# FAVOR attention and a bilinear FFN on one core: weights fetched by another queue, the second addend of a weight product added by VectorE, and a re-ordered lead-in

## The chip, the cores and the metric

The kernel runs on one core of one Trainium2 chip. The metric is the device time of one launch in microseconds (us). The engines are TensorE (PE; its weight loads are shown apart as PEld), VectorE (DVE), ScalarE (ACT), GpSimd (POOL) and SyncE (SP). SP does no arithmetic here: it only issues DMAs. ACT does arithmetic and issues some DMAs too. A queue issues its DMAs in the order of the program, and one that has to wait holds up those behind it.

## The reference

The reference is attention with random features, followed by a feed-forward product with a bilinear gate. There are 8 batches of 8 heads, 576 tokens, 64 numbers per head and 128 features.

```python
def phi(x):                                   # x = q or k, scaled by 1/64**0.25
    proj = np.einsum('bhsd,md->bhsm', x, omega)
    h = proj - np.sum(x * x, axis=-1, keepdims=True) / 2.0
    return np.exp(h - np.max(h, axis=-1, keepdims=True)) / np.sqrt(m)
kv = np.einsum('bhsm,bhsd->bhmd', phi(k_s), v)
z = np.sum(phi(k_s), axis=2)
num = np.einsum('bhsm,bhmd->bhsd', phi(q_s), kv)
den = np.einsum('bhsm,bhm->bhs', phi(q_s), z)[..., None] + 1e-06
x = (num / den).transpose(0, 2, 1, 3).reshape(4608, 512)
out = (((x @ w1) * (x @ w2)) @ w3) @ w_out    # w1, w2: 512x1024; w3: 1024x1024; w_out: 1024x512
```

The four weight matrices arrive as 64-bit floats, q, k, v and omega as 32-bit floats.

## The kernel before, in words

**Tiling.** The 4608 tokens are 36 chunks of 128. For a chunk, `k_chunk` makes the features of k and `kv_batch` sums them with v once all chunks of a batch are there (tile `kvp`). `q_chunk` makes the features of q (projection `qpj`, exponential `qe`, fp16 pair `eq`) and has them transposed by DMA (`eqT`). `q_attend` multiplies them by `kv` (tile `nu`) and divides; `x_turn` makes a pair of fp16 numbers of the row and has it transposed by DMA (`xT`). `gate` computes `x@w1` and `x@w2` (tile `ab`) and their product, and `project_out` multiplies by W (tile `o`) and stores. W = w3·w_out is computed once on the chip, in fp32 (`W_block`, tile `wp`): 1024 rows in eight blocks, and since w_out arrives in two parts of 512 rows, W's first halves of the sums are kept in `Wb` and the second halves are added later. That addition is a matmul of the kept block by a unit matrix, `ident`, into the same sum (L616); ACT then copies the sum back (L630).

**Precision.** An fp32 matmul shows as two records in the profile. Elsewhere numbers go as pairs of fp16 (a high and a low part) in three passes (`PASSES`). The first five chunks of q and the first ten of k (`QF`, `KF`) are projected in fp32 whole, L287; later ones are first split into pairs.

**The weights' lead-in.** The 20 units of weights (the letters of `ORDER`: o is w_out, W is w3, 1 and 2 are w1 and w2; a, b and S are the splits that follow) hold 1 MB each. A unit takes these steps: the fetch, a DMA of ACT's queue (L526); the magnitude, an Abs on ACT (L534); the bits, four operations on DVE that put a 32-bit float together from the two words (L540, L542, L543, L545); and then the product on PE with its copy (`W`), or the sums of magnitudes (`1`, `2`). There are three buffers for raw words, so the fetch of a unit waits until the bits of the unit three earlier are done, and two buffers for magnitudes.

**What sets the order.** A plan of slots. Each chunk begins three slots after the one before (`PACE`), each piece is put into a slot with a rank (`put`), `PER` says how many steps of the weights go into a slot, `LAGS`, `KVD`, `KOFF`, `VB`, `NOFF` and `QOFF` shift single pieces, and `RESERVE` is the number of units of gates that are held back as filling. The framework then orders the instructions of each engine by the order in which they were written and by when it thinks their inputs are there. `EH`, `EL`, `QH`, `QL` and `DQ` pick engines for the high and low parts and the form of the exponential (for one form, '1', eight small operations with the maximum as bias on ACT; for '0', one addition on DVE and one exponential). At its start the program loads omega (L205, L206, into the first block of `Wb`), two chunks of k and, soon, two of q, all by SP's queue (L228). The rows of v come by SP's queue as well (L351), and so do the transposes (L427, L481).

## The time and the profile before

| | |
|---|---|
| three runs | 848.72, 844.92 and 849.43 us; median 848.72 us |
| the profiled execution | 844.82 us, of which the span is 843.0 us |
| mean granted clock of TensorE | 0.977 |
| PE busy | 786.0 us, 93% of the span |
| DVE busy | 577.0 us, 68% |
| ACT busy | 437.6 us, 52% |
| POOL busy | 228.5 us, 27% |
| the first output projection begins | 187.65 us |

The rows of the profile are read thus. A group has its line, engine, operation and tiles, the number of instructions, then their busy time in us and the mean of one in ns, and behind the next bar the idle time of the engine just before them, with what ended it. A row of the timeline has the start and the length in us, then engine, line, operation, tiles and the number of instructions run together, and in brackets the idle time before. A row of the windows has the two ends and the length of the stretch, then for PE, PEld, DVE, ACT and POOL the busy us with the instructions in parentheses, then TensorE's granted clock, the busy share of the DMA engines and the GB/s that they moved.

### The profile page before, as it was taken

The numbers are of one execution on the slowest core, as the hardware profiler recorded it, in microseconds if no ns is written. First come the engines' busy times: TensorE is split into PE (matmuls) and PEld (weight loads), VectorE is DVE, ScalarE is ACT, GpSimd is POOL, SyncE is SP. The second block draws the span as 40 slices with busy tenths as digits, with TensorE's granted clock in tenths as the row PEclk, the third lists the DMA queues.
The fourth block names the chain that finished last, engine by engine and source line by source line (L and its number), as shares of the span: only waits on it lengthen the run. The fifth ranks groups of instructions, "written<-read, shape, count | busy, mean of one in ns | idle before, by whom it ended". The sixth has DMA issues, their size and how long they took to land.

```text
span 843.0 us, 19911 instructions
## 1 busy us (share of the span) xinstructions
PE 786.0 (93%) x8353; PEld 580.1 (69%) x8353; DVE 577.0 (68%) x1049; ACT 437.6 (52%) x793; POOL 228.5 (27%) x210
## 2 busy tenths in 40 slices
PE   1968799799979999999999999999999999999998
PEld 1436455696858777777777777777777777777773
DVE  5695967886888788768777877787778765452000
ACT  2674746884655557656555565466545433232221
POOL 0000001221435324533333334333433332221110
PEclk8889699999989999999999999999999999999999
DMA  8584659334435454535343634354333342321000
GB/s 302 187 267 145 200 151 213 89 64 72 114 93 115 73 153 89 101 76 126 91 87 81 137 85 87 79 126 101 78 84 67 65 85 66 76 51 38 26 14 37
DMA packets 142521, 88.38 MB, mean 105 GB/s; under 512 B 116704, under 2 KB 116832, under 8 KB 142432
## 3 DMA queue, kind: packets, MB, share of 16 engines
q1 hardware_dynamic: 134944, 66.15, 35.8%
q10 hardware_dynamic: 7488, 20.97, 7.6%
q8 instruction: 65, 1.06, 0.5%
q14 instruction: 24, 0.20, 0.1%
HBM read 49.35 MB, written 9.44 MB: 70 GB/s over the span
## 4 chain that ended last, share of the span: by engine, by line
PE 46%; DVE 16%; ACT 9%; issue 7%; DMA 1%; POOL 1%; SPq 0%; DVEq 0%; ACTq 0%; POOLq 0%
PE ab L678 24%; PE o L707 15%; DVE nm L306 3%; PE kvp L411 3%; DVE khl L155 2%; DVE ke L320 2%; PE nu L440 2%; DVE qe L320 2%; ACT ek L143 2%; ACT qe L321 1%; PE qpj L294 1%; DVE xs L455 1%; DMA kraw<-kT 1%; DVE asb L688 1%; ACT xhl L476 1%
## 5 line engine op out<-in xcount | busy, mean ns | idle before, releaser
L678 PE MATMUL ab<-xT,w12b 128*128 128x256 f16 (+1 forms) x3840 | 390.7, 262 | 5.7 <-DMA xT<-xhl 4.7
L678 PEld LDWEIGHTS <-w12b 128*128 128x128 f16 x3840 | 340.1, 98 | 43.5 <-issue 4.9
L707 PE MATMUL o<-Wb,arena 128*128 128x512 f16 x864 | 195.7, 383 | 1.0 <-DVE p2p L195 1.0
L693 POOL TENSOR_TENSOR arena<-asb,arena 128x512 f16<-128x512 f32 x72 | 92.8, 1288 | 316.0 <-ACT arena L692 316.0
L707 PEld LDWEIGHTS <-arena 128*128 128x128 f16 x864 | 82.3, 98 | 98.1 <-issue 4.2
L688 DVE TENSOR_TENSOR asb<-ab,asb 128x512 f32<-128x512 f32 x72 | 49.5, 687 | 115.9 <-PE ab L678 91.8
L330 POOL TENSOR_TENSOR eq<-qe,eq 128x1024 f16<-128x1024 f32 x34 | 74.5, 2192 | 135.0 <-DVE eq L141 80.6
L618 PE MATMUL wp<-w12b 128*128 128x512 f32 x128 | 64.6, 656 | 12.5 <-DVE w12b L545 12.4
L330 POOL TENSOR_TENSOR ek<-ke,ek 128x1024 f16<-128x1024 f32 x26 | 56.6, 2179 | 70.9 <-ACT ek L143 62.5
L692 ACT CAST arena<-asb 128x512 f16<-128x512 f32 x72 | 44.1, 612 | 58.0 <-DVE asb L688 57.9
L155 DVE SCALAR_TENSOR_TENSOR qhl<-qraw,s,qhl 128x512 f16<-128x512 f32 x31 | 51.4, 1657 | 18.1 <-ACT qhl L152 18.1
L687 ACT ACTIVATE asb<-ab 128x512 f32<-128x512 f32 x72 | 42.3, 587 | 34.7 <-PE ab L678 30.9
L321 ACT ACTIVATE qe<-qe,ln_e,es 128x1024 f32<-128x1024 f32 x31 | 38.4, 1238 | 41.2 <-DVE qe L320 41.1
L321 ACT ACTIVATE ke<-ke,ln_e,es 128x1024 f32<-128x1024 f32 x26 | 32.2, 1238 | 51.1 <-DVE ke L320 51.1
L476 ACT ACTIVATE xhl<-xs,p2r 128x512 f16<-128x512 f32 x36 | 26.0, 721 | 62.1 <-DVE p2r L198 60.3
L618 PEld LDWEIGHTS wp<-w12b 128*128 128x128 f32 x128 | 26.2, 210 | 45.7 <-issue 30.7
L306 DVE TENSOR_REDUCE nm<-kpj 128x8 f32<-128x1024 f32 x36 | 43.8, 1217 | 9.8 <-PE kpj L287 5.1
L711 ACT ACTIVATE o<-o,oscs 128x512 f32<-128x512 f32 x36 | 24.3, 675 | 40.8 <-PE o L707 33.6
L411 PE MATMUL kvp<-vhl,ek 128*128 128x65 f16 (+1 forms) x880 | 41.8, 208 | 3.4 <-DVE xs L455 3.4
L306 DVE TENSOR_REDUCE nm<-qpj 128x8 f32<-128x1024 f32 x36 | 43.7, 1215 | 0.2
L440 PE MATMUL nu<-kv,eqT 128*128 128x65 f16 (+1 forms) x960 | 34.1, 195 | 8.4 <-DMA eqT<-eq 7.6
L141 DVE CAST eq<-qe 128x1024 f16<-128x1024 f32 x31 | 21.5, 692 | 29.0 <-ACT qe L321 29.0
(121 smaller groups left out, 929.2 us busy)
## 6 DMA issues: line engine op xcount, KB each, us to landing
kraw<-kT SPq DMA_DIRECT2D x36, 256.0 KB, 2.8
qraw<-qT SPq DMA_DIRECT2D x36, 256.0 KB, 2.7
vraw<-v SPq DMA_DIRECT2D x36, 256.0 KB, 4.3
out<-o SPq DMA_DIRECT2D x36, 256.0 KB, 2.3
arena<-w3T ACTq DMA_DIRECT2D x8, 1024.0 KB, 6.5
arena<-w ACTq DMA_DIRECT2D x8, 1024.0 KB, 6.2
arena<-wo ACTq DMA_DIRECT2D x4, 1024.0 KB, 5.1
eqT<-eq SPq DMA_TRANSPOSE x72, 3.1
```

The lines of the kernel that those rows point to most:

```text
L155: nc.vector.scalar_tensor_tensor(lo, src, s, hi, ALU.mult, ALU.subtract)
L306: nc.vector.tensor_reduce(nm, pj, AX.X, ALU.max, negate=True)
L321: nc.scalar.activation(e, e, AF.Exp, scale=es, bias=ln_e)
L330: (nc.vector if lo == "d" else nc.gpsimd).tensor_tensor(t[:, 1], e, t[:, 0], ALU.subtract)
L411: nc.tensor.matmul(ps[:, h // 4, h % 4], x, y, start=n == 0, stop=n == len(mm) - 1)
L440: nc.tensor.matmul(nu[r0:r1, h // 4, h % 4], t[:, x, place(h), r0:r1], kvs[b][:, y, h], start=n == 0, stop=n == 2,)
L618: nc.tensor.matmul(ps, w[:, j, k * P : (k + 1) * P], guest[:, j], start=j == j0, stop=j == HALF - 1,)
L678: nc.tensor.matmul(ps[:, k], w12[m][i][cc][:, a, r * P : (r + 1) * P], x[:, b, cc, off : off + T], start=j == 0, stop=j == len(mm) - 1,)
L688: nc.vector.tensor_tensor(asb, ab[1], asb, ALU.mult)
L692: nc.scalar.copy(h[:, 0], asb)
L693: nc.gpsimd.tensor_tensor(h[:, 1], asb, h[:, 0], ALU.subtract)
L707: nc.tensor.matmul(ps, hs[c, f][0][:, a], W[f][:, b], start=i == 0, stop=i == len(mm) - 1)
```

## The change

1. **Fetches.** The 20 fetches of weights are issued by SP's queue (`FQ = 's'`). The first unit, of w_out, is fetched in two DMAs, and its Abs and its bits are done in halves (`cuts`). The loads of k's chunks 0 and 1 are issued by ACT's queue instead.
2. **Early Abs.** An Abs of one column is the first arithmetic of ACT (`T0`).
3. **Omega** has a tile of its own, and its split is put into slot 0 instead of slot 4 (`OM_AT`).
4. **W's second addend** is added by DVE, straight from the sum to `Wb` (`WADD`): the eight matmuls by `ident` and eight of the sixteen copies on ACT go.
5. **v's scaling** (ten operations) goes from DVE to ACT (`V_ACT`).
6. **Whole projections**: q's chunk 5 and k's chunk 10 are projected in fp32 as well (`QF`, `KF`).
7. **Order**: q's first two loads wait for the second unit's bits (`QD`); priorities for pieces (`PR`); and new tables `PER`, `PACE`, `LAGS`, `KVD`, `KOFF`, `VB`, `NOFF`, `QOFF` and `RESERVE`, with the tables that pick engines. `MS`, `KFIRST` and `OM1` stand at values that change nothing.

```diff
-EH = 'aaaaaadadadada'
-EL = 'ddddddpdpdppppp'
-QH = 'aaaaad'
-QL = 'ddp'
-DQ = '111110000000'
-QF = 5
-KF = 10
-V_ACT = 0
+EH = 'aaaaaddadaaadaaaaaaaaaa'
+EL = 'ddppddpdpddpppppppppppppppp'
+QH = 'aaaaaaddd'
+QL = 'ddpdppppppppppp'
+DQ = '101110010000000000000000000'
+QF = 6
+KF = 11
+V_ACT = 1
+PR = {'vscale': 100, 'norm': 400, 'split': 100, 'bits': -100, 'x': 50}
+START = 1
+WADD = 1
+FQ = 's'
+T0 = 1
+CH = 1
+QD = 1
...
-PER = [3, 1, 0, 1, 0, 1, 1, 0, 1, 0, 1, 1, 0, 1, 1, 0, 0, 1, 1, 1, 1, 1, 1, 1, 1, 1, 1, 1, 1, 1, 1, 1, 1]
-PACE = {13: 2}
+PER = [3, 1, 0, 1, 0, 1, 1, 0, 1, 0, 1, 1, 0, 1, 1, 0, 0, 1, 1, 1, 1, 1, 1, 1, 0, 3, 0, 1, 1, 1, 1, 1, 2]
+PACE = {13: 3, 11: 3}
...
-RESERVE = 3
+RESERVE = 2
...
-OM_AT = 4
+OM_AT = 0
...
-    om_raw = Wb[:, 0, 0:M]
-    nc.sync.dma_start(om_raw[0:D], omT)
-    nc.sync.dma_start(om_raw[D:P], omT)
+    om_raw = const.tile([P, M], F32, name="om_raw")
+    if OM1 == 0:
+        nc.sync.dma_start(om_raw[0:D], omT)
+        nc.sync.dma_start(om_raw[D:P], omT)
...
+    if T0:
+        nc.scalar.activation(om_sq, ln_e, AF.Abs)
...
-    def load(src, c, name):
+    def load(src, c, name, queue=nc.sync):
...
-        nc.sync.dma_start(t, src[c])
+        dma = queue.dma_start(t, src[c])
...
+        if name == "q" and c < 2 and QD >= 0:
+            tc.add_manual_dep(
+                dma.ins,
+                converted[QD].name,
...
-            nc.scalar.dma_start(raw.rearrange("p (j i) -> p j i", j=src.shape[1]), src)
-            st["raw"] = raw.rearrange("p (i t) -> p i t", t=2)
+            raw = raw.rearrange("p (j i) -> p j i", j=src.shape[1])
+            step = src.shape[1] // cuts
+            for k in range(0, src.shape[1], step):
+                {'a': nc.scalar, 's': nc.sync, 'p': nc.gpsimd}[pick(FQ, nfetch[0])].dma_start(raw[:, k : k + step], src[:, k : k + step])
...
-            nc.scalar.activation(st["g"], st["raw"][:, :, 1].bitcast(F32), AF.Abs)
+            for a in pieces:
+                nc.scalar.activation(st["g"][:, a], st["raw"][:, a, 1].bitcast(F32), AF.Abs)
...
-        return from_float64(lambda: dst, src, f"wo_{j}")
+        return from_float64(lambda: dst, src, f"wo_{j}", cuts=1 if n or not START else 2)
...
-                if j0:
+                if j0 and not WADD:
                     nc.tensor.matmul(ps, ident, Wb[:, i + k + 1], start=True, stop=False)
...
-                nc.scalar.copy(Wi, ps)
+                if j0 and WADD:
+                    nc.vector.tensor_tensor(Wi, ps, Wi, ALU.add)
+                else:
+                    nc.scalar.copy(Wi, ps)
...
-    for u in units[:RAW64_BUFS]:
+    for n, u in enumerate(units[:RAW64_BUFS]):
         u[0]()
         u[0] = None
+        if START and n < 2:
+            load(kT, n, "k", nc.scalar)
...
-    for c in range(2):
+    for c in range(0 if START else KFIRST, 0 if START else 2):
         load(kT, c, "k")
```

Three places show how the tables and queues move instructions. The first is SP's queue from the start of the program (`kraw`, `qraw` and `vraw` are the loads of a chunk of k, q and v; `arena` holds the raw weights). Before:

```order
L205 DMA Wb<-omT 64x128
L206 DMA Wb<-omT 64x128
L228 DMA kraw_104<-kT 128x512
L228 DMA kraw_106<-kT 128x512
L228 DMA qraw_338<-qT 128x512
L228 DMA qraw_359<-qT 128x512
L228 DMA kraw_163<-kT 128x512
L228 DMA kraw_210<-kT 128x512
L351 DMA vraw_176<-v 128x512
```

and now:

```order
L226 DMA om_raw<-omT 64x128
L227 DMA om_raw<-omT 64x128
L568 DMA arena<-wo 128x1024 x2
L568 DMA arena<-wo 128x2x1024
L568 DMA arena<-w3T 128x4x512
L568 DMA arena<-w 128x2x1024
L257 DMA kraw_155<-kT 128x512
L568 DMA arena<-w3T 128x4x512
L387 DMA vraw_184<-v 128x512
```

Here the weights have moved into the same line as k, q and v: the fetch of the fourth unit (w) stands ahead of the third load of k, and that load ahead of the fifth unit.

The second place is DVE in the middle of the lead-in: `kpj` is the projection of a chunk of k, `vhl` the scaled v, L155 (L175 now) the low half of a split of w1, `ws` its scale. The first row before is the last step of the seventh unit, and what follows lies ahead of the eighth:

```order
L545 SCALAR_TENSOR_TENSOR w12b<-arena 128x1024
L306 TENSOR_REDUCE nm<-kpj_316 128x8
L388 TENSOR_SCALAR vhl_1_340<-vraw_178,s_3_283 128x8x64
L316 TENSOR_SCALAR nm<-nm 128x8
L388 TENSOR_SCALAR vhl_2_361<-vraw_180,s_3_283 128x8x64
L388 TENSOR_SCALAR vhl_3_374<-vraw_182,s_3_283 128x8x64
L155 SCALAR_TENSOR_TENSOR w12b<-w12b,ws 128x512
L306 TENSOR_REDUCE nm<-kpj_378 128x8
L388 TENSOR_SCALAR vhl_4_400<-vraw_184,s_3_283 64x8x64
```

Now (the two L592 are the last steps of the eighth and of the ninth unit):

```order
L342 TENSOR_REDUCE nm<-kpj_321 128x8
L215 TENSOR_SCALAR p2p_4_300<-l1m 128x1
L592 SCALAR_TENSOR_TENSOR w12b<-arena 128x1024
L218 RECIPROCAL p2r_4_302<-p2p_4_300 128x1
L352 TENSOR_SCALAR nm<-nm 128x8
L584 TENSOR_SCALAR arena<-arena 128x1024
L638 TENSOR_SCALAR ws<-p2r_4_302 128x1
L586 TENSOR_SCALAR arena<-arena 128x1024
L589 SCALAR_TENSOR_TENSOR arena<-arena 128x1024
L175 SCALAR_TENSOR_TENSOR w12b<-w12b,ws 128x512
L592 SCALAR_TENSOR_TENSOR w12b<-arena 128x1024
```

The scalings of v are gone from between the units, and three of the four low halves of the split and one of the two reductions of `kpj` have moved behind the ninth unit; before, all four halves and both reductions stood ahead of the eighth unit's last step.

The third place is PE ahead of the first gate (`wp` is a block of W, `qpj` and `kpj` the projections of a chunk of q and of k, `ab` the gate). Before:

```order
L618 MATMUL wp_0_675<-w12b 128x512 x2
L287 MATMUL kpj_651<-Wb,kraw_387 128x128 x8
L618 MATMUL wp_0_675<-w12b 128x512 x2
L618 MATMUL wp_1_681<-w12b 128x512 x4
L287 MATMUL qpj_816<-Wb,qraw_488 128x128
L678 LDWEIGHTS w12b
L678 MATMUL ab_0_0_693<-xT_619,w12b 128x128
```

and now:

```order
L670 MATMUL wp_0_664<-w12b 128x512
L670 MATMUL wp_1_669<-w12b 128x512 x4
L323 MATMUL qpj_813<-om_raw,qraw_496 128x128 x8
L323 MATMUL kpj_853<-om_raw,kraw_526 128x128 x8
L670 MATMUL wp_0_694<-w12b 128x512 x4
L670 MATMUL wp_1_699<-w12b 128x512 x4
L733 LDWEIGHTS w12b
L733 MATMUL ab_0_0_710<-xT_690,w12b 128x128
```

Two projections and a second pair of W's blocks now stand between the first pair and the gate; before, that pair came behind the gate.

More of the change, by code (lines that the diff above doesn't have):

```diff
@@ L1 @@
 import math
-from contextlib import ExitStack
+from contextlib import ExitStack, nullcontext
 import concourse.bass as bass
@@ L114, in tile_favor_attention_then_bilinear_ffn, with ahead, early, go @@
     TOK = GROUP * P
+    def ahead(kind):
+        return tc.high_priority(offset=PR[kind]) if PR.get(kind) else nullcontext()
+    def early(kind, fn):
+        def go(*args):
+            with ahead(kind):
+                return fn(*args)
+        return go
     const = ctx.enter_context(tc.tile_pool(name="const", bufs=1))
@@ L339, in k_chunk @@
             ek[c] = e
-        if c == 0:
+        if c == 0 and K_BEHIND >= 0:
             with tc.issue_after(converted[K_BEHIND]):
@@ L533, in magnitude, with words @@
             st["dst"] = new()
-            nc.scalar.activation(st["g"], st["raw"][:, :, 1].bitcast(F32), AF.Abs)
-        def bits():
-            g = st["g"]
-            top, low = st["raw"][:, :, 1], st["raw"][:, :, 0]
-            nc.vector.tensor_scalar(g, g, F64_TOP, F64_LEAST, ALU.min, ALU.max)
-            g = g.bitcast(U32)
-            nc.vector.tensor_scalar(g, g, 3, 0x3FFFFFFF, ALU.logical_shift_left, ALU.bitwise_and)
-            nc.vector.scalar_tensor_tensor(g, top, 0xC0000000, g, ALU.bitwise_and, ALU.bitwise_or)
-            converted.append(
-                nc.vector.scalar_tensor_tensor(
-                    st["dst"].bitcast(U32), low, 29, g, ALU.logical_shift_right, ALU.bitwise_or
-                ).ins
-            )
+            for a in pieces:
+                nc.scalar.activation(st["g"][:, a], st["raw"][:, a, 1].bitcast(F32), AF.Abs)
+        def words():
+            for a in pieces:
+                g, dst = st["g"][:, a], st["dst"][:, a].bitcast(U32)
+                top, low = st["raw"][:, a, 1], st["raw"][:, a, 0]
+                nc.vector.tensor_scalar(g, g, F64_TOP, F64_LEAST, ALU.min, ALU.max)
+                g = g.bitcast(U32)
+                nc.vector.tensor_scalar(
+                    g, g, 3, 0x3FFFFFFF, ALU.logical_shift_left, ALU.bitwise_and
+                )
+                nc.vector.scalar_tensor_tensor(
+                    g, top, 0xC0000000, g, ALU.bitwise_and, ALU.bitwise_or
+                )
+                last = nc.vector.scalar_tensor_tensor(
+                    dst, low, 29, g, ALU.logical_shift_right, ALU.bitwise_or
+                )
+            return last
+        def bits():
+            with tc.issue_after(converted[-1]) if 0 < len(converted) < CH else nullcontext():
+                last = words()
+            converted.append(last.ins)
             raw_at.append(st["at"])
             mag_at.append(st["mag"])
-        return [fetch, magnitude, bits]
+        return [fetch, early("mag", magnitude), early("bits", bits)]
     l1s = {}
@@ L621, in product @@
                         guest[:, j],
-                        start=j == j0,
+                        start=j == (0 if WADD else j0),
                         stop=j == HALF - 1,
@@ L636, in W_block @@
             product,
-            keep,
+            early("keep", keep),
         ]
@@ L723, in v_batch @@
         cs = chunks_of(b)
-        v_work.extend((b, lambda n=n: v_norm(b, n)) for n in range(len(cs)))
-        v_work.append((b, lambda: v_scale(b)))
-        v_work.extend((b, lambda n=n: v_split(b, n)) for n in range(len(cs)))
+        v_work.extend((b, early("vnorm", lambda n=n: v_norm(b, n))) for n in range(len(cs)))
+        v_work.append((b, early("vscale", lambda: v_scale(b))))
+        v_work.extend((b, early("vsplit", lambda n=n: v_split(b, n))) for n in range(len(cs)))
     def v_unit():
@@ L761, in tile_favor_attention_then_bilinear_ffn @@
         units.append([None] * 3 + st + [None] if len(st) == 1 else st + [None] * (5 - len(st)))
-    for u in units[:RAW64_BUFS]:
+    for c in range(KFIRST):
+        load(kT, c, "k")
+    for n, u in enumerate(units[:RAW64_BUFS]):
         u[0]()
         u[0] = None
+        if START and n < 2:
+            load(kT, n, "k", nc.scalar)
     behind = sorted(range(5), key=lambda k: -SKEW[k])
@@ L791, in ready @@
     def ready(c):
-        x_turn(c)
+        early("x", x_turn)(c)
         for c0, m in groups:
@@ L797, in ready @@
                     need = [(n, u // m) for n in range(2)]
-                    units.append((need, lambda c0=c0, m=m, u=u: gate(c0, m, u)))
+                    units.append((need, early("gate", lambda c0=c0, m=m, u=u: gate(c0, m, u))))
                 for k, f in enumerate(behind_by):
                     units.insert(2 + 3 * k, f)
-                behind_by[:] = [(["k"], lambda c=c: project_out(c)) for c in range(c0, c0 + m)]
+                behind_by[:] = [
+                    (["k"], early("out", lambda c=c: project_out(c))) for c in range(c0, c0 + m)
+                ]
                 queue.extend(units)
```

54 lines of the change are left out of this document (35 added, 19 removed).

## The prediction, as put on record

> **What bounds the kernel now.** I read the windows first, cut where the work changes: the start, the weights up to the first kv sum, the stretch to the first gate, from there to the first output projection, and the rest. Columns: the ends and length of the stretch, busy us of PE, PEld, DVE, ACT and POOL, TensorE's granted clock, DMA share, GB/s.
>
> ```profile
> 0.00:21.50 21.50, 3.51 (x33) 3.33 (x33) 12.45 (x27) 5.03 (x6) 1.43 (x12) 0.87 0.89 303
> 21.50:77.00 55.50, 47.52 (x198) 26.49 (x199) 40.39 (x62) 34.93 (x78) 0.52 (x1) 0.90 0.58 196
> 77.00:106.50 29.50, 19.89 (x115) 11.28 (x115) 26.51 (x43) 19.34 (x49) 0.47 (x5) 0.77 0.68 208
> 106.50:187.60 81.10, 75.17 (x798) 56.47 (x797) 60.40 (x126) 57.23 (x129) 12.47 (x15) 1.00 0.58 130
> 187.60:300.00 112.40, 105.10 (x1374) 80.37 (x1375) 91.00 (x169) 64.95 (x108) 40.15 (x34) 0.97 0.46 98
> 300.00:760.00 460.00, 455.53 (x5263) 347.40 (x5262) 336.66 (x607) 240.32 (x398) 163.06 (x134) 1.00 0.42 89
> ```
>
> From 300 us on PE is busy for 455.5 of 460 us: what is won earlier is kept there, and nothing more can be won. Up to 187.6 us PE is idle for 41.5 us: 18.0 in the start, 8.0, 9.6 and 5.9 in the next three. Both orders have issued the same work of PE by the first output projection, but for eight matmuls; so the sum is made at that one milestone, 187.65 us. The timeline gives the marks on the way and the groups of the first 188 us the durations.
>
> ```profile
> 8.86 0.69 DVE L540 TENSOR_SCALAR arena<-arena 128x1024 f32<-128x1024 f32 x1 [7.78 <-ACT arena L534]
> 21.54 9.42 PE L618 MATMUL wp<-w12b 128*128 128x512 f32 x16 [8.36 <-DVE w12b L545]
> 40.14 1.60 PE L287 MATMUL kpj<-Wb,kraw 64*128 64x128 f32 x22
> 62.16 7.13 PE L618 MATMUL wp<-w12b 128*128 128x512 f32 x16 [2.17 <-DVE w12b L545]
> 69.13 8.15 PE L411 MATMUL kvp<-vhl,ek 128*128 128x65 f32 x72
> 88.41 0.29 PE L440 MATMUL nu<-kv,eqT 128*128 128x65 f16 x2 [6.63 <-DMA eqT<-eq]
> 106.56 5.52 PE L678 MATMUL ab<-xT,w12b 128*128 128x128 f16 x96 [2.34 <-DMA xT<-xhl]
> 187.65 1.25 PE L707 MATMUL o<-Wb,arena 128*128 128x512 f16 x5
> ```
>
> Until 62 us PE waits for the last step of the bits on DVE, L545: the first block of W at 21.54, the fourth (ninth unit) at 62.16. After that it waits for transposes: 6.63 us for `eqT`, 2.34 us for `xT`.
>
> ```profile
> L618 PE MATMUL wp<-w12b 128*128 128x512 f32 x128 | 64.6, 656 | 12.5 <-DVE w12b L545 12.4
> L616 PE MATMUL wp<-Wb,ident 128*128 128x512 f32 x16 | 8.4, 616 | 0.0
> L540 DVE TENSOR_SCALAR arena<-arena 128x1024 f32<-128x1024 f32 x20 | 14.4, 719 | 17.8 <-ACT arena L534 17.8
> L542 DVE TENSOR_SCALAR arena<-arena 128x1024 uint32<-128x1024 uint32 x20 | 13.8, 690 | 0.4
> L543 DVE SCALAR_TENSOR_TENSOR arena<-arena 128x1024 uint32<-128x1024 uint32 x20 | 24.4, 1220 | 0.4
> L545 DVE SCALAR_TENSOR_TENSOR w12b<-arena 128x1024 uint32<-128x1024 uint32 x20 | 24.3, 1220 | 6.2 <-PE wp L618 5.9
> L306 DVE TENSOR_REDUCE nm<-kpj 128x8 f32<-128x1024 f32 x10 | 12.2, 1217 | 5.1 <-PE kpj L287 5.1
> L155 DVE SCALAR_TENSOR_TENSOR w12b<-w12b,ws 128x512 f16<-128x512 f32 x16 | 12.1, 757 | 2.5 <-ACT w12b L152 2.5
> L388 DVE TENSOR_SCALAR vhl<-vraw,s 128x512 f32<-128x512 f32 (+1 forms) x10 | 4.4, 478 | 0.1
> L581 DVE TENSOR_REDUCE l1m<-l 128x1 f32<-128x512 f32 x4 | 2.7, 684 | 0.0
> L316 DVE TENSOR_SCALAR nm<-nm 128x8 f32<-128x8 f32 x14 | 2.3, 164 | 0.0
> ```
>
> One unit's bits take 0.719 + 0.690 + 1.220 + 1.220 = 3.85 us of DVE.
>
> **The lead-in's order: −5 us.** Before, DVE does this from 8.86 us to the end of the ninth unit, 62.1 us: nine units 34.6, five reductions of `kpj` 6.1, one `l1m` 0.7, four low halves of a split 3.0, five scalings of v 2.4, and some 20 small operations like L316, 0.15 us each, 3.0: 49.8 of 53.3 us, so 3.5 us of waits. Now the scalings are ACT's, three of the halves and one reduction stand behind the ninth unit: 34.6 + 4.9 + 0.7 + 0.8 + 3.0 = 44.0 us. With the same start and the same waits the ninth unit ends at 8.9 + 44.0 + 3.5 = 56.4 us. Behind it on PE stand its product, 7.1 us, and 80 records of the kv sum; before, 72 took 8.15 us, so 80 take 9.1: it ends at 72.6 us instead of 77.3, 4.7 us sooner. PE sets a second bound. Its first block of W now comes behind a third projection of k, and by the order of DVE after three units, two reductions and three steps of the fourth: 8.9 + 11.5 + 2.4 + 2.6 = 25.4 us instead of 21.5. From there it has the 47.5 us of the second window less the projection done ahead (1.60 us for 22 records, so 1.2 for 16), 46.3: 71.7 us. Both bounds lie close; I take −5. If DVE's waits vanish PE binds, −5.6; if 5 us of waits are added, 0.
>
> **The start: 0.** The early Abs and the half-sized first unit would bring DVE's start of 8.86 us forward.
>
> ```profile
> 6.41 1.28 ACT L534 ACT_TABLE_LOAD   x1 [6.41 <-DMA arena<-wo]
> 7.71 1.12 ACT L534 ACTIVATE arena<-arena 128x1024 f32<-128x1024 f32 x1
> 10.54 0.29 ACT L169 ACTIVATE junk_om<-Wb 128x128 bf16<-128x128 f32 x1
> ```
>
> The table's load is 1.28 us, half an Abs 0.56: −1.8 us. Omega's split now stands ahead of the bits and costs about that much again: a Square of 0.29 us on ACT, a small matmul, and on DVE five operations, four of them small like L316. I keep 8.9 us, with −1.8 and +1 as bounds.
>
> **W's second addend: −6.9 us.** Sixteen records of L616 go. Warm, their weight loads follow each other by 0.43 us:
>
> ```profile
> 126.07 0.19 PEld L616 LDWEIGHTS wp<-Wb,ident 128*128 128x128 f32 x1 [0.24 <-issue]
> 126.50 0.19 PEld L616 LDWEIGHTS wp<-Wb,ident 128*128 128x128 f32 x1 [0.24 <-issue]
> L688 DVE TENSOR_TENSOR asb<-ab,asb 128x512 f32<-128x512 f32 x5 | 3.4, 687 | 5.1 <-PE ab L678 5.1
> ```
>
> 16 × 0.43 = 6.9 us, on an engine that is 93% busy in the fourth window, where 12 of the 16 stand; the busy time of the group, 8.4 us, is the upper bound. In their place come eight additions of the kind of L688, 8 × 0.69 = 5.5 us, while the scalings of v take 4.4 us off DVE: 1.1 us more in all. The cover is DVE's idle time, 110.6 − 86.9 = 23.7 us in the third and fourth windows. A block's banks come free after DVE's addition instead of ACT's copy; what stands ahead of that addition is at most a unit's remaining steps, and if half of the eight wait for one of 1.2 us with nothing beside them, the saving is 4.
>
> **From the kv sum to the first output projection: −3 us.** PE's idle time there is 15.5 us. Ahead of the first `nu` (6.63 us of waiting) stands one more projection of q, 1.2 us. Between the first pair of blocks and the gate now stand two projections and eight products more, so the 2.34 us for `xT` are filled. −3.5, and 0.5 back because the first gate's fillers are then missing further on. Bounds: −5 (half of what is left), and +4 if a transpose is late by one unit's bits, since SP's queue now holds weights.
>
> **After it: 0.** One more chunk of q and one of k are projected in fp32: 16 records, 1.2 us, where 24 of fp16 stood, 1.5 us by the 20 below; I count nothing for it. One wait of 3.7 us stands there, and the new tables may remove or repeat it: with the smaller waits beside it −5 to +6.
>
> ```profile
> 243.32 0.28 PE L294 MATMUL qpj<-om,qhl 64*128 64x128 f16 x4 [3.67 <-ACT qhl L152]
> 245.77 1.25 PE L294 MATMUL kpj<-om,khl 64*128 64x128 f16 x20 [0.68 <-DVE mx L468]
> ```
>
> **The fetches: 0 by themselves**, since DVE, not the landing, ends PE's waits up to 62 us. What they cost ACT:
>
> ```profile
> L526 ACTq DMA_DIRECT2D arena<-w3T x8: 374/374/418, 6.0 to 101.0; - x8
> 14.25 3.07 SPq L351 DMA_DIRECT2D vraw<-v  x5
> 14.32 0.39 ACTq L526 DMA_DIRECT2D arena<-w  x1
> 23.03 1.12 ACT L534 ACTIVATE arena<-arena 128x1024 f32<-128x1024 f32 x1 [7.60 <-DMA arena<-w]
> ```
>
> 0.37 us an issue, 7.5 us for all twenty, on an engine busy for 116.5 of the first 187.6 us. The fourth unit, issued at 14.32 together with five loads of v, is there at 23.0. The Trainium skill (DMA: Bandwidth & Descriptors, Issuing engines are not separate DMA queues) says that DMAs started by different engines run on the same 16 DMA engines, and that another issuer saves only the issuing. The DMA share of 0.89 in the first window agrees; by that rule edit 1 is worth 0 on the path, as in my sum. The same page (Queues, rings and completion order) says that a DMA engine takes turns between queues by packets; by that, the fourth unit, now ahead of the loads of v in one line, would land some us sooner, which no run here shows yet.
>
> **The sum.** −5 + 0 − 6.9 − 3 + 0 + 0 = −14.9 on the profiled 844.82 us: 829.9. The runs shown lie 0.1 to 4.6 above the profiled one, on average 2.9: 833 us. With all bounds on the good side, −5.6 − 1.8 − 8.4 − 5 − 5 = −25.8, it is 822; on the bad side, 0 + 1 − 4 + 4 + 6 = +7, 855.
>
> **The rivals.**
> - *Everything fits* (0.15): DVE starts 1.8 us earlier, its waits vanish, and the 3.67 us go: −14.9 − 1.8 − 0.6 − 3.7 = −21.0, 827. For it: DVE's waits are only 3.5 us. Against: 20 fetches in the line of k, q and v.
> - *Only the matmuls count* (0.20): the ninth unit comes sooner, but what was moved behind it (three low halves, one reduction: 3.5 us) and the eight additions fall due before the first gate, where DVE is 26.5 of 29.5 us busy. Then −6.9 alone: 841. For it: that window.
> - *DVE is the bound of the whole lead-in* (0.10): it works 139.8 of 187.6 us, its total hardly changes, and PE only waits elsewhere: 0, 848.
> - *One line* (0.11), slower: SP's queue has now a fetch that waits for a raw buffer, that is for a unit's bits, ahead of loads of k and transposes, and loads that wait for PE ahead of fetches.
>
> ```profile
> SPq L228 <- PE kpj L287: 29.9, 7, 18.5
> SPq L427 <- ACT eq L143: 9.1, 3, 4.8
> ```
>
> Loads of k already wait 29.9 us for their buffers (7 times) in that queue, and transposes 9.1 us; before, no weight stood behind them. If five waits reach PE, each of a unit's bits and an issue, 3.85 + 0.37, that is +21 against −14.9: 854. It decides from 3.6 such waits on.
>
> **Chances.** Forecast 0.44, rivals 0.15, 0.20, 0.10, 0.11. A measurement here tells no less than 0.5%: faster is below 844.5, slower above 853. Forecast and first rival are faster, and most of the second (0.16): 0.75; same 0.04 + 0.10 = 0.14; slower 0.11. The range leaves out the last rival and the edges: 820 to 848; the forecast's own is 828 to 838.
>
> **What would show it.** The ninth unit's product of W at 56 us instead of 62.16 and the first kv sum's end at 72; no rows of `ident`, and first output projection at 173 instead of 187.65; PE's idle time before it down by 8 us; DVE's additions near 0.69 us; the waits of SP's queue without long ones at the fetches. Wrong would be: a first block of W after 27 us, PE waits for `eqT` or `xT` above 5 us each, the projection later than 180, or new idle time of PE beyond 300 us.

## The result, and the profile after

The changed kernel takes 817.22 us (median of four runs, 816.96 to 818.14) against 848.36 us before: ratio 0.9642, 95% interval 0.9613 to 0.967. That is 31 us less; forecast were 15 less, 833 us, with 820 as the lower end. The profiled execution has a span of 815.5 us instead of 843.0, so 27.5 of the 31 us can be followed in the traces; the other 3.6 are there because the profiled execution of before, 844.82 us, lies below all four of its other times. Of e2 and e5 below, one run each (834.26 and 838.78 us) was in a slower state and is left out of the medians.

At the prediction's marks:

| | before | forecast | after |
|---|---|---|---|
| first block of W begins | 21.5 | 25.4 | 24.5 |
| last bits of the ninth unit end | 62.1 | 56.4 | 51.9 |
| first kv sum ends | 77.3 | 72.6 | 68.1 |
| first gate begins | 106.6 | | 99.4 |
| first output projection begins | 187.65 | 172.8 | 165.04 |
| from there to the end of the span | 655.4 | 655.4 | 650.5 |
| PE idle up to the first output projection | 41.5 | 33.5 | 27.4 |

The windows of the kernel after, cut at its own marks (columns as in the prediction):

```profile
0.00:24.50 24.50, 7.05 (x50) 5.96 (x50) 17.60 (x37) 12.31 (x31) 1.43 (x12) 1.00 0.88 312
24.50:68.00 43.50, 43.50 (x184) 24.66 (x185) 37.93 (x54) 35.02 (x70) 0.60 (x2) 1.00 0.78 273
68.00:99.40 31.40, 25.40 (x156) 14.04 (x154) 29.45 (x48) 21.53 (x53) 2.01 (x6) 0.89 0.75 205
...
165.04:815.50 650.46, 638.58 (x7196) 483.04 (x7195) 403.86 (x792) 326.28 (x543) 201.43 (x176) 1.00 0.37 84
```

Between the first block of W and the end of the kv sum PE now has no idle time at all, at a granted clock of 1.00; before it was idle for 8.0 us there at 0.90. So the 47.5 us that the prediction took as PE's work in that stretch held some slow matmuls: less the 1.2 us of a projection that is now done ahead it is 43.5 us, not 46.3.

The timeline of the kernel after, at the first block of W, the fourth, the first kv sum, the first gate and the first output projection:

```profile
24.48 10.17 PE L670 MATMUL wp<-w12b 128*128 128x512 f32 x16 [1.21 <-DVE w12b L592]
52.10 7.13 PE L670 MATMUL wp<-w12b 128*128 128x512 f32 x16
59.07 9.04 PE L447 MATMUL kvp<-vhl,ek 128*128 128x65 f32 x80
99.41 2.90 PE L733 MATMUL ab<-xT,w12b 128*128 128x128 f16 x49
165.04 1.04 PE L762 MATMUL o<-Wb,arena 128*128 128x512 f16 x4
```

PE no longer waits at the fourth block, and not for `xT` at the first gate. Why DVE is ten us earlier with the ninth unit is seen in the windows from its first bits to the end of the ninth unit's, before and then after:

```profile
8.86:62.11 53.25, 36.20 (x144) 18.81 (x144) 45.55 (x72) 31.15 (x73) 0.00 (x0) 0.84 0.73 243
```

```profile
7.52:51.91 44.39, 31.15 (x117) 15.66 (x115) 40.23 (x61) 31.59 (x68) 0.00 (x0) 1.00 0.85 298
```

DVE (45.55 and 40.23 us) starts 1.3 us sooner, has 5.3 us less to do and is idle for 4.2 us instead of 7.7. The largest of its waits before is gone; it stood ahead of the reduction of a projection of k:

```profile
41.35 1.22 DVE L306 TENSOR_REDUCE nm<-kpj 128x8 f32<-128x1024 f32 x1 [4.07 <-PE kpj L287]
```

Its waits for an Abs are no shorter in this stretch, 3.0 us before and 3.5 after. They fell ahead of it and behind it. Up to the first output projection they were (us in total, times, longest), before and then after:

```profile
DVE arena L540 <- ACT arena L534: 17.8, 10, 7.8
```

```profile
DVE arena L584 <- ACT arena L577: 4.7, 6, 3.3
```

Of these 13.1 us, 7.6 lie at the very start, where omega's split now comes first and DVE's first bits come 1.3 us sooner; behind the ninth unit 7.0 us became 1.0. An Abs waits for its fetch, and the fetch for its buffer, which is free once the bits of the unit three earlier are done. The timeline of before, for the seventh unit: its buffer is free at 28.26 (the last bits of the fourth), its fetch goes out at 36.02, 7.8 us later.

```profile
27.03 1.23 DVE L545 SCALAR_TENSOR_TENSOR w12b<-arena 128x1024 uint32<-128x1024 uint32 x1
36.02 0.37 ACTq L526 DMA_DIRECT2D arena<-w3T  x1
41.06 1.14 ACT L534 ACTIVATE arena<-arena 128x1024 f32<-128x1024 f32 x1 [1.42 <-DMA arena<-w3T]
```

After, for the eighth unit: free at 30.62, fetched at 30.68.

```profile
29.39 1.23 DVE L592 SCALAR_TENSOR_TENSOR w12b<-arena 128x1024 uint32<-128x1024 uint32 x1
30.68 0.37 SPq L568 DMA_DIRECT2D arena<-w  x1
```

Over the fetches from the fourth on, the time from the buffer's being free to the issue (call it the lateness; it is the difference of two such rows for each unit) adds up to 89.3 us before, 5.3 on average, and 4.0 us after, 3.1 of it in one fetch that stood behind two transposes and a load of q. (The 1.9 in the expectation of e5 takes three fetches that the timeline runs together in one row as evenly spaced.)

### The profile page after: what moved, and what is told of

Read it like the earlier page. It is cut to its first block, busy times and chain, and to the rows that moved or that the text cites. A ratio compares the mean times of both kernels' runs of the same rounds, so it can differ in the third digit from the quotient of the medians.

```text
span 815.5 us, 19863 instructions
## 1 busy us (share of the span) xinstructions
PE 776.2 (95%) x8320; PEld 578.9 (71%) x8320; DVE 544.9 (67%) x1045; ACT 443.6 (54%) x793; POOL 213.4 (26%) x208
## 4 chain that ended last, share of the span: by engine, by line
PE 84%; DVE 6%; DMA 4%; ACT 3%; issue 2%; SPq 0%; ACTq 0%; DVEq 0%
PE ab L733 42%; PE o L762 21%; PE wp L670 7%; PE kvp L447 5%; PE nu L476 3%; PE qpj L330 2%; PE kpj L330 2%; DMA kraw<-kT 1%; DMA arena<-wo 1%; DVE nm L342 1%; DVE khl L175 1%; DMA arena<-w 1%; ACT qe L354 1%; DVE w12b L592 1%; DVE arena L589 1%
## 5 line engine op out<-in xcount | busy, mean ns | idle before, releaser
L762 PE MATMUL o<-Wb,arena 128*128 128x512 f16 x864 | 192.4, 379 | 1.9 <-ACT asb L742 1.9
L748 POOL TENSOR_TENSOR arena<-asb,arena 128x512 f16<-128x512 f32 x72 | 84.7, 1176 | 279.8 <-ACT arena L747 272.7
L366 POOL TENSOR_TENSOR eq<-qe,eq 128x1024 f16<-128x1024 f32 x33 | 70.3, 2130 | 147.4 <-DVE eq L161 80.6
L366 POOL TENSOR_TENSOR ek<-ke,ek 128x1024 f16<-128x1024 f32 x25 | 53.3, 2130 | 87.7 <-ACT ek L163 87.1
L670 PE MATMUL wp<-w12b 128*128 128x512 f32 x128 | 62.9, 647 | 3.3 <-DVE w12b L592 3.3
L357 ACT ACTIVATE qe<-qe,ln_e,es 128x1024 f32<-128x1024 f32 x29 | 35.9, 1239 | 44.9 <-DVE qe L356 44.9
L175 DVE SCALAR_TENSOR_TENSOR qhl<-qraw,s,qhl 128x512 f16<-128x512 f32 x30 | 26.9, 898 | 33.2 <-ACT qhl L172 33.2
L513 DVE SCALAR_TENSOR_TENSOR xhl<-xs,p2r,xhl 128x512 f16<-128x512 f32 x36 | 28.3, 787 | 27.7 <-ACT xhl L512 27.5
L766 ACT ACTIVATE o<-o,oscs 128x512 f32<-128x512 f32 x36 | 24.5, 680 | 37.8 <-PE o L762 37.8
L189 ACT ACTIVATE junk_q<-qraw 128x512 bf16<-128x512 f32 x30 | 18.8, 627 | 45.5 <-DMA qraw<-qT 45.5
```

Of the source, the lines that this page charges most:

```text
L175: nc.vector.scalar_tensor_tensor(lo, src, s, hi, ALU.mult, ALU.subtract)
L357: nc.scalar.activation(e, e, AF.Exp, scale=es, bias=ln_e)
L366: (nc.vector if lo == "d" else nc.gpsimd).tensor_tensor(t[:, 1], e, t[:, 0], ALU.subtract)
L670: nc.tensor.matmul(ps, w[:, j, k * P : (k + 1) * P], guest[:, j], start=j == (0 if WADD else j0), stop=j == HALF - 1,)
L748: nc.gpsimd.tensor_tensor(h[:, 1], asb, h[:, 0], ALU.subtract)
L762: nc.tensor.matmul(ps, hs[c, f][0][:, a], W[f][:, b], start=i == 0, stop=i == len(mm) - 1)
```

## The experiments

The kernel before took 845.6 to 848.1 us (medians) beside these runs, so what is said to be so many us above the changed kernel's 817.2 holds to about 1.5 us. The framework makes the order of every engine anew when a queue or a wait is changed, so such a run changes more than its one line.

### Which queue fetches

**e1: ACT's queue again.**

```diff
-FQ = 's'
+FQ = 'a'
```

> The changed kernel with all fetches of weights back in ACT's queue, all else as changed. Theory F (new, after the result): a fetch waits in the line of its issuer for a raw buffer, that is for DVE's bits, and on ACT it holds up the Abs and exponentials behind it, which DVE then waits for; so DVE's waits for Abs (4.7 us up to the first output projection, 17.8 before) grow by 5 us or more, the fourth kv-side mark (end of the first kv sum, 68.1 us) comes 3 to 8 us later and the time is 821 to 826. Theory D (the prediction's own step, fetches worth 0): only 7.5 us of issuing come back to ACT, marks within 1.5 us, 816 to 819.

Measured: 845.94 us (843.75 to 849.38, ten runs), ratio to before 0.9982 (0.9954 to 1.001). This one edit undoes the whole gain, 28.7 us, several times what theory F gave. The lateness is back at 85.9 us in sum, the ninth unit's product begins at 66.2 us instead of 52.1. In its waits DVE has these (first the Abs, then the low half of the kv sum), PE the third:

```profile
DVE arena L584 <- ACT arena L577: 12.9, 8, 3.9
DVE kv L451 <- ACT kv L450: 12.2, 1, 12.2
...
PE wp L670 <- DVE w12b L592: 17.6, 4, 12.0
```

Its timeline shows how a fetch gets late: it stands in ACT's line behind an instruction that waits for PE, here the copy of the kv sum.

```profile
84.38 0.61 ACT L450 ACTIVATE kv<-kvp 128x520 f16<-128x520 f32 x1 [12.27 <-PE kvp L447]
...
85.08 0.38 ACTq L568 DMA_DIRECT2D arena<-w3T  x1
...
86.96 1.12 ACT L577 ACTIVATE arena<-arena 128x1024 f32<-128x1024 f32 x1
```

The buffer of that fetch had been free since 70.0 us. Of the 17 fetches, 14 went out 2 us or more after their buffer was free, so it is mostly ACT that holds up the fetches, not, as theory F had it, the fetches ACT. One reservation: PE's order differs in a few places and those of DVE and ACT in more, so order and queue are not quite apart.

**e5: POOL's queue.** Here PE works on its tiles in the same order as in the changed kernel, and DVE and ACT nearly so.

```diff
-FQ = 's'
+FQ = 'p'
```

> The changed kernel with the fetches of weights in POOL's queue: the orders of PE, DVE and ACT stay nearly those of the changed kernel, and the fetches share no line with ACT's work nor with the loads of k, q and v. Theory L (a fetch is issued late when the line of its issuer stands at something else: ACT's fetches went out 85.9 us late in sum in the first run, SP's 1.9): POOL hardly works in the lead-in, so the lateness stays under 10 us in sum and the time is 815 to 821. Theory S (it is the one line of SP that helps, weights ahead of the loads of v): the time is 824 or more.

Measured: 831.4 us, 14 us above the changed kernel; the three runs lie far apart (826.2 to 836.7, the profiled one is the longest), so the size is rough. The lateness is small, 8.9 us in sum, as theory L asked, and the time is theory S's: being issued on time is not enough. The transfers from 13 to 25 us in this kernel, and from 11 to 20 us in the kernel after (DMA issues: KB each, median us to landing):

```profile
vraw<-v SPq DMA_DIRECT2D x5, 256.0 KB, 6.1
arena<-w POOLq DMA_DIRECT2D x1, 1024.0 KB, 9.5
arena<-w3T POOLq DMA_DIRECT2D x1, 1024.0 KB, 10.0
```

```profile
vraw<-v SPq DMA_DIRECT2D x5, 256.0 KB, 5.7
arena<-w SPq DMA_DIRECT2D x1, 1024.0 KB, 5.9
arena<-w3T SPq DMA_DIRECT2D x1, 1024.0 KB, 5.1
```

From POOL's queue a unit takes 9.5 to 10 us to land beside the five loads of v in SP's, from SP's own, ahead of them, 5 to 6. The first block of W begins at 31.2 us instead of 24.5. The Trainium skill (DMA: Bandwidth & Descriptors, Queues, rings and completion order) says that a DMA engine takes turns between queues, a packet at a time; the rows agree, since two queues share the bandwidth where one serves the weights first. The same skill (SBUF — State Buffer, SBUF: two separate sides) says that a DMA of POOL's queue is prepared by POOL's own cores, which some of DVE's operations can lock out. The traces do not need this for the two units: in the kernel before the same two, from ACT's queue, landed after 8.7 and 10.1 us beside the same five loads, and later fetches of POOL's queue (at 31.7, 37.9 and 44.9 us) after 5.9 to 6.1 us.

**e8: SP's queue, but a unit late.** Every fetch from the fourth on also waits for the bits of the unit two earlier.

```diff
+                if n >= 3:
+                    tc.add_manual_dep(dma.ins, converted[n - 2].name, ..., reason="late")
```

> The changed kernel, SP's queue kept, but every fetch from the fourth on waits for the bits of the unit two earlier instead of three, so it goes out later by one unit's bits (3.85 us and what stands between). Theory L: the same loss as with ACT's queue, because the lateness is the same (about 5 us a fetch): 835 to 850. Theory C (what costs in ACT's queue is that ACT itself is held up by waiting fetches): nothing holds ACT up here, 817 to 825.

Measured: 837.64 us (836.69 to 838.12), 20.4 above the changed kernel, with nothing of it in ACT's line. The lateness is 128 us in sum, DVE's waits for Abs are 18.1 us up to the first output projection. Theory L stands: late fetches cost most of what ACT's queue costs, without ACT's line. The orders of PE, DVE and ACT were made anew here too; e5, with PE's order kept, shows that weights that arrive later cost much by themselves.

**e6: the kernel before, fetching by SP.**

```diff
-            nc.scalar.dma_start(raw.rearrange("p (j i) -> p j i", j=src.shape[1]), src)
+            nc.sync.dma_start(raw.rearrange("p (j i) -> p j i", j=src.shape[1]), src)
```

> The kernel before with one line changed: the fetches of weights in SP's queue. Theory L: the lateness of 89.3 us in sum falls below 25, the end of the first kv sum comes 5 us or more sooner than 77.3, and the time is 8 to 20 us below before's 848. Theory O (the moved fetches pay only with the new order): SP's line of before has loads of k and q that wait for PE ahead of the fetches, the lateness stays, and the time is 843 to 855.

Measured: 845.86 us (843.25 to 849.18, ten runs), ratio 0.9993 (0.9965 to 1.0021): no difference, theory O, and not for its reason. The lateness did fall, to 2.5 us, and the ninth unit's product came at 57.5 us instead of 62.2. But the product then took 9.3 us instead of 7.1, at a granted clock of 0.76 instead of 1.00, and half of the rest went into the next wait of the old order, on PE:

```profile
87.13 0.30 PE L440 MATMUL nu<-kv,eqT 128*128 128x65 f16 x2 [7.86 <-DMA eqT<-eq]
```

Before, this wait was 6.63 us at 88.41. The first output projection begins at 186.3 us, 1.4 sooner.

### The order

**e4: the old tables in the changed kernel** (`PER`, `PACE`, `LAGS`, `KVD`, `KOFF`, `VB`, `NOFF`, `QOFF`, `RESERVE` as before, `PR = {}`).

```diff
-PR = {'vscale': 100, 'norm': 400, 'split': 100, 'bits': -100, 'x': 50}
+PR = {}
-PER = [3, 1, 0, ..., 0, 3, 0, 1, 1, 1, 1, 1, 2]
+PER = [3, 1, 0, ..., 1, 1, 1, 1, 1, 1, 1, 1, 1]
...
-RESERVE = 2
+RESERVE = 3
```

> The changed kernel with the tables of the order of before (PER, PACE, LAGS, KVD, KOFF, VB, NOFF, QOFF, RESERVE) and no priorities; the edits of the code stay. Theory A (edits carry the lead-in): the first kv sum ends within 3 us of 68.1, the saved matmuls stay, and only the steady part loses: 820 to 826. Theory B (the order carries half or more of the 31 us): 830 to 842, with waits of PE for eqT or xT above 5 us ahead of the first output projection.

Measured: 834.43 us (831.68 to 837.02), 17.2 above the changed kernel: theory B's size, without its waits (PE's longest for a transpose ahead of the first output projection is 2.7 us; its longest behind the first kv sum, 7.9, is for DVE's bits). But the first kv sum ends at 68.5 us, as theory A had it; 6.5 us are lost between it and the first output projection (171.9 us) and 7.5 behind that. The steady part, from 300 us on:

```profile
300.00:750.00 450.00, 444.50 (x5121) 339.05 (x5119) 325.47 (x586) 234.66 (x389) 159.72 (x132) 1.00 0.41 88
```

PE is idle for 5.5 us there, as it was before (4.5); in the changed kernel it is not idle at all from 300 to 737 us.

**e7: the new tables in the kernel before**, and **e9: with SP's queue as well** (the line of e6).

```diff
-PER = [3, 1, 0, ..., 1, 1, 1, 1, 1, 1, 1, 1, 1]
+PER = [3, 1, 0, ..., 0, 3, 0, 1, 1, 1, 1, 1, 2]
...
-RESERVE = 3
+RESERVE = 2
```

> The kernel before with the new tables of the order alone (PER, PACE, LAGS, KVD, KOFF, VB, NOFF, QOFF, RESERVE). Theory A (tables are worth 13 to 17 us by themselves, as the old tables in the changed kernel cost 17): 831 to 836. Theory B (they fit the changed kernel's fetches only): 843 to 853.

> The kernel before with both: fetches in SP's queue and the new tables (no other edit). Alone they gave 2 and 10 to 12 us. Theory X (they need each other, as the loss of 28.7 us with ACT's queue in the changed kernel suggests): together 18 us or more, 822 to 830, with the first output projection at 172 to 178. Theory Y (they add): 832 to 836.

Measured: 835.88 us (834.67 to 836.85) and 833.70 us (831.67 to 835.88). The tables give 10 to 12 us by themselves: the first output projection comes 4.0 us sooner and what follows it is 6.2 us shorter. SP's queue adds 2 at most. In the kernel before the two do not help each other (theory X falls), so what makes the queue worth so much is in the other edits.

**e10: `PACE` and `RESERVE` of before**, and **e3: the last `NOFF` of before.** Both change the order only behind the first output projection.

```diff
-PACE = {13: 3, 11: 3}
-RESERVE = 2
+PACE = {13: 2}
+RESERVE = 3
```

```diff
-NOFF = [2, 2, 2]
+NOFF = [2, 2, 1]
```

> The changed kernel with PACE and RESERVE of before; the order changes only behind the first output projection. Theory R: the 4.9 us won there (655.4 to 650.5) are these two numbers', by the units of gates held back: 821 to 825, the first output projection unchanged at 165 to 166. Theory N: something else in the tables: 816 to 819.

> The changed kernel with NOFF's last number back to 1, which only moves the splits of q and k by a slot, in the steady part. Theory P: the 4.9 us that the span won after the first output projection come from the splits no longer running beside POOL (the low halves L175 took 0.75 to 0.9 us, L155 before 1.5 to 2.1); with the old slot they take over 1.4 us on average again, DVE's busy time grows by 20 us or more, and the time is 3 to 6 us longer, 820 to 823. Theory Q: the same slow splits, but hidden behind PE's work: the time within 1.5 us, 816 to 819.

Measured: e10 822.79 us, but from 817.85 to 824.69; e3 817.80 us (816.87 to 818.62). In e10's profiled execution 3.2 us are lost behind the first output projection and 4.2 ahead of it, where nothing was changed (below, under what was not expected); its fastest run is 0.9 us above the changed kernel's fastest, so e10 is not clear. e3 tests nothing of theory P: only ACT's order changed in it, and the low halves of q's splits took 0.82 us, as in the changed kernel, so the slot does not bring back the low halves of before.

### The other edits, one at a time, with SP's queue

**e2: the second addend by `ident`.**

```diff
-WADD = 1
+WADD = 0
```

> The changed kernel with W's second addend again by eight matmuls with ident and ACT's copies. The prediction's term: +6.9 us (4 to 8.4), so 821 to 826, 824 likeliest, all of it between the end of the first kv sum and the first output projection. Rival: additions hold DVE up there, so undoing them gives DVE 5.5 us back and the cost is under 3 us, 817 to 820.

Measured: 821.55 us (819.55 to 826.38), 4.3 above. The first output projection is 6.3 us later, as the term of 6.9 had it; some 2 us of it are made good behind that.

**e11: without the edits of the start; e12: v's scaling on DVE; e16: only omega's split later.**

```diff
-START = 1
-T0 = 1
-CH = 1
-QD = 1
-OM_AT = 0
+START = 0
+T0 = 0
+CH = 0
+QD = -1
+OM_AT = 4
```

e12 and e16 have one line each:

```diff
-V_ACT = 1
+V_ACT = 0
```

```diff
-OM_AT = 0
+OM_AT = 4
```

> The changed kernel without the edits of the start: first unit whole, loads of k in SP's queue, no early Abs, omega's split in slot 4, no waits of q's first loads. The prediction's term for the start was 0, with -1.8 and +1 as bounds: 816 to 820. Rival (the first block of W is what the lead-in hangs on, and DVE's start 1.3 us sooner counts twice, because PE then runs without a gap at its full clock): 821 to 826.

> The changed kernel with v's scaling on DVE again (ten operations, 4.4 us). By the prediction, half of them ahead of the ninth unit, 2.4 us, and the rest covered: 818 to 821. Rival (DVE is the bound all the way to the first output projection): 821 to 823; other rival (covered by PE's own work, which now runs without gaps): 816.5 to 818.

> The changed kernel with omega's split back in slot 4, all else as changed. In the profile after, the split stands ahead of the first Abs (ACT 5.03 to 6.9 us) and of DVE's first bits (7.52 us). Theory: the bits start about 1 us sooner and the time is 815 to 817. Rival: the first loads land no sooner than now, and it is the same, 817 to 819, or slower where the split falls between units.

Measured: e11 826.20 us (825.92 to 826.35), 9.0 above, the rival's size; e12 822.9 us (820.8 to 827.2), 5.7 above; e16 818.57 us (815.61 to 819.99), not to be told from the changed kernel (DVE's first bits come at 8.0 us in it, not sooner). In e11 the first block of W begins at 20.9 us, sooner than in the changed kernel, and the first output projection at 174.0, nine later: a sooner first block is not what the edits of the start bring. In e12 the first output projection comes at 170.3 us. No single undoing gave a kernel faster than the changed one.

### What the queue's worth hangs on

**e15: ACT's queue and the old tables; e13: ACT's queue, v on DVE; e14: ACT's queue, no edits of the start; e17 and e18: neither v on ACT nor the edits of the start, with SP's and with ACT's queue.** The edits are those above, together; the first three with this line, the last two as e11 and e12 in one, e18 with this line too.

```diff
-FQ = 's'
+FQ = 'a'
```

> The changed kernel with fetches in ACT's queue and the old tables, no priorities: the fourth corner beside 817.2 (SP, new), 845.9 (ACT, new) and 834.4 (SP, old). Theory H (the new tables are written for fetches on time and lose with late ones): 836 to 846, no slower than with the new tables. Rival (tables and queue add): 858 to 868.

> The changed kernel with fetches in ACT's queue and v's scaling on DVE again. With SP's queue the scaling on DVE cost 5.7 us. Theory F (ACT's line is full: what stands in it delays fetches, so an ACT with less work issues them sooner): the loss of ACT's queue, 28.7 us, falls to 5 to 18 above the 822.9 of v on DVE: 828 to 841, and the lateness below 65 us in sum. Rival (the lateness comes from waits in ACT's line, not from work): 843 to 852.

> The changed kernel with fetches in ACT's queue and without the edits of the start (loads of k in SP's queue again, no halves, no early Abs, omega's split later). With SP's queue the edits of the start were worth 9.0 us (826.2 without). Theory G (they help only when fetches come on time; with late fetches the early start is lost at the next fetch): 840 to 847, no worse than with them. Rival (worth 9 us in either case): 852 to 857.

> The changed kernel without the edits of the start and with v's scaling on DVE, fetches in SP's queue. Alone these two cost 9.0 and 5.7 us; if they add, 831.9, so 828 to 835. Theory J (what SP's queue is worth hangs on these two edits): this run and the next differ by under 10 us. Rival (it hangs on something else): they differ by 20 us or more.

> As the run before, with fetches in ACT's queue. Undoing each alone gave 3.0 and 5.2 us there; if they add, 845.9 - 8.2 = 837.7, so 834 to 841. Theory J: within 10 us of the run before. Rival: 850 or more.

Measured medians, us:

| | SP's queue | ACT's queue | difference |
|---|---|---|---|
| changed kernel | 817.2 | 845.9 (e1) | 28.7 |
| with the old tables | 834.4 (e4) | 858.5 (e15) | 24.1 |
| v on DVE | 822.9 (e12) | 840.7 (e13) | 17.8 |
| no edits of the start | 826.2 (e11) | 842.9 (e14) | 16.7 |
| neither of the two | 823.5 (e17) | 839.5 (e18) | 16.1 |
| kernel before, new tables | 833.7 (e9) | 835.9 (e7) | 2.2 |
| kernel before | 845.9 (e6) | 846.1 (same chip) | 0.3 |

Tables and queue nearly add (e15 fell to its rival). Theory F's time held in e13 (840.7 us), but not its lateness, 77.5 us in sum instead of under 65; theory G held in e14; e17 lies 8 us below the sum of its two losses, e18 where the sum had it. Two edits do not add: v's scaling on ACT and the edits of the start gain 6.2 us together with SP's queue (e17 to the changed kernel), nothing or less each alone (e12 and e11 against e17), and lose 6.4 together with ACT's queue (e18 to e1). Both put work or loads into ACT's line; they pay with the fetches out of it, and then only both together. That the shared line is the reason is argued, not shown. The two edits make up 12.6 of the 28.7 us. Theory J was half right: without them 16.1 us are left, not under 10. Which of the edits that remain (the additions on DVE, the priorities, omega's own tile, the whole chunks, the engines' tables) lifts the queue's worth from under 3 to 16 us stays open. The lateness alone does not say it: 102.6 us in sum (e7) and 4.5 (e9) lie 2.2 us apart in time.

## Why the prediction was wrong, step by step

**The fetches, 0 by themselves: the step that failed.** As an edit of the kernel before the fetches are worth nothing (e6), but in the sum with the other edits they are worth 28.7 us (e1), and no term held that. The zero was argued from what PE waits for (DVE's last bits) and not followed on to what DVE waits for, nor to when a fetch goes out. The row of L540, 17.8 us of waiting for Abs, stood in the prediction, and DVE's waits were carried into the forecast as "the same waits", while fetches went out 5.3 us late on average. Without that lateness the ninth unit's product came 4.7 us sooner even in the old order (e6); with it put back in SP's queue 20 us were lost (e8), and with weights that land later, PE's order kept, 14 (e5). The Trainium skill (DMA: Bandwidth & Descriptors, Issuing engines are not separate DMA queues) was quoted for the zero; that another issuer saves only the issuing does not hold in the changed kernel, because the issuer's line decides when the DMA goes out and ahead of which others. The other half of that paragraph came true, but had no price in the sum: ahead of the loads of v, the fourth and fifth unit landed after 5.9 and 5.1 us instead of 8.7 and 10.1.

**The lead-in's order, −5: it was −9.2.** The mechanism was right, the ninth unit's bits set the kv sum. The same start and waits were wrong. The prediction reckoned 49.8 us of work and 3.5 of waits for DVE before; the window has 45.6 busy and 7.7 idle (the rows of one engine overlap, by 0.1 us at 14.14 us, so a sum of durations is too long). After, it has 40.2 busy and 4.2 idle. So of the 10.2 us that the bits end sooner, 5.3 are less work, where 5.8 were forecast, 1.3 are the start and 3.5 are waits, two terms that were put at nothing; one us is given back, since 80 records of the kv sum stand behind the ninth unit instead of 72. The good bound, −5.6, was PE's, and was too small because PE's busy time of before was taken at a granted clock of 0.90.

**The start, 0.** In place of it stand the 9.0 us of e11, but of the sooner bits themselves 1.3 us. With v's scaling on DVE the same edits bring only 0.6 (e17 and e12), so most of the 9.0 is how they fit the other edits, which a term for the start alone could not hold.

**W's second addend, −6.9.** Right in place and size at its mark (6.3 us in e2; the additions take 0.686 us each where 0.69 were reckoned), 4.3 us at the end. The group of the kernel after:

```profile
L683 DVE TENSOR_TENSOR Wb<-wp,Wb 128x512 f32<-128x512 f32 x8 | 5.3, 686 | 3.3 <-PE wp L670 3.3
```

**From the kv sum to the first output projection, −3 beside the matmuls.** Measured: 110.35 to 96.9 us, 13.4 less; taking the 6.9 off leaves 6.5. PE's idle time there fell from 15.5 to 9.9 us. The covers named in the prediction did what they should: the wait for `eqT` at the first `nu` is gone, and the gate's for `xT`. With the old tables the stage is 6.5 us longer (e4), about half of its gain.

**After it, 0: it was −4.9.** The runs show that the tables do it, with 4.5 to 8.0 us between old and new tables in each of four pairs of kernels (before and e7, e6 and e9, e4 and the changed kernel, e15 and e1); the 0 came from taking PE's 99% busy time from 300 us on as the end of what can be won. Nearly all of the 4.9 lay in that last per cent, in PE's waits from 300 us on, none of which is left after (before, us in total, times, longest):

```profile
PE kvp L411 <- DVE xs L455: 3.4, 3, 1.7
PE kpj L294 <- DVE xs L455: 1.1, 1, 1.1
```

**The rivals.** "Everything fits", 827 us, came nearest, with chance 0.15; its mechanism is what the trace shows in part: DVE starts 1.3 us sooner, its waits are nearly halved, and the wait of 3.67 us is gone, though others came in its place (PE is idle for 7.3 us from the first output projection to 300 us before, for 8.1 after). It was still 10 us short. "One line" is refuted, though SP does wait at its fetches (47.6 us in sum, longest 7.2): in its queue the lateness is 4.0 us in sum, and no wait of PE for a transpose up to the first output projection is longer than 2.7 us. Late loads did turn out to decide, but in ACT's line, where the weights came from. "DVE is the bound" and "only the matmuls count" fell with the marks.

**The range.** All bounds on the good side gave 822 us, and 817 was measured. Of the gap, 2.9 us are the offset that the prediction added for runs above the profiled one; after, the profiled run lies at the median. Two terms passed their bounds: the lead-in with the start, −9.2 against −7.4, and the stage behind, −6.5 against −5. The terms were bounded as if each stood for itself, while the experiments show that the queue's worth changes with the other edits.

## What to carry to other kernels

Here fetches that wait for a buffer went out on time from a queue whose engine does no arithmetic, and 5 us late behind ACT's work. For each prefetch, compute the time from the buffer's being free to the issue, and take a large sum of it as a candidate before asking who waits on the chain; what it is worth has to be measured, since it was 28.7 us in one kernel and under 3 in another. Edits that share an engine's line can have the opposite sign with and without each other, so a term for each alone does not add up; price them with the queue that they will meet. And where one cause can move several terms at once, bounds made for each term alone are too narrow.
